# Attention loads issued in pairs of turns with a sixth home, and two weight rows converted later

## The chip, the cores and the metric

The kernel runs on one core of a Trainium2 chip. The metric is the device time of one execution in microseconds; the median of three runs is compared. One more execution was taken with a profile, and all rows below come from it.

## What is computed

Retention attention over 4 batches, 8 heads, 576 positions and head size 64, and behind it two feed-forward blocks on the 2304 tokens (model width 512, hidden width 2048), the first with a leaky ReLU whose slope is learnt, the second with a GELU in its sigmoid form:

```python
scores = scale * np.matmul(q, k.transpose(0, 1, 3, 2))
Dmat = np.where(rel >= 0, gamma[:, None, None] ** rel[None, :, :], 0.0)
ret = scores * Dmat[None, :, :, :]
attn = np.matmul(ret, v)
...
h = x @ w_in
g = np.maximum(h, 0.0) + alpha * np.minimum(h, 0.0)
x = g @ w_out
...
h = x @ w_in
g = h * (1.0 / (1.0 + np.exp(-1.702 * h)))
out = g @ w_out
```

The weights arrive as 64-bit floats in two 32-bit words each. The kernel puts them together itself and splits each value into a high and a low part, so that three products (high times high, high times low, low times high) replace one product in full precision.

## The kernel before

**Attention.** The 16 pairs of heads are worked on in turns, one pair a turn, in the loop `for i in range(n_a + 1)`; turn 16 only finishes pair 15. In turn `i` TensorE multiplies queries with keys (`a_scores`, tile `sc`), sums the keys' outer products with the values into a state (`a_outer`, tile `st`, needs the keys `kts` that ScalarE scaled in `a_keys` a turn before), and multiplies the scores of pair `i - 1` with its values (`a_within`, tile `av`). In an even turn it also does the last block of pairs `i` and `i + 1` (`a_tail`, which needs the inputs `ld` of pair `i + 1`) and adds the part that comes from earlier blocks for the two pairs before (`a_across`, tile `avt`). ScalarE takes the states out (`a_states`), and copies the finished outputs (`a_out`); VectorE multiplies the scores with the decay (`a_evac`), combines the states (`a_sums`), and for the first eight pairs writes the low part of the outputs (`a_rests`).

**Loads.** Each pair has two transfers on SyncE's queue: its inputs `ld` (864 KB; one of five homes, list `LOADS`), and its keys once more in another layout, `kts` (256 KB; one of eight places). `a_load` is called once a turn, four turns ahead. A home comes free when `a_across` has read its pair, which happens two pairs at a time in even turns; SyncE takes its instructions in order, so a transfer whose home is still in use holds up all behind it. The trace shows SyncE also waiting before an issue until a transfer eight places earlier has landed.

**Weight rows.** The first block's weights come in 16 rows. Row `m` is loaded in two pieces (`w_load`, `w_piece`, tile `raw`, two slots: `m % 2`) and converted by six instructions: ScalarE's `w_abs` (line 118, writes `cv`), VectorE's `w_clamp` (two instructions, lines 122 and 125), `w_top` (132) and `w_low` (139), ScalarE's `w_hi` (line 85, writes the high part of `w`), VectorE's `w_lo` (line 90, writes its low part). The third of every three products of a row needs the low part. A table of times says in which turn, or later in which step, each of these instructions is written into the program: `rows` for rows 0 to 2, `pace` for rows 3 to 15; `run_to(t)` emits what is due. Engines run their instructions in that order.

**First block.** Behind the attention, steps follow (`steps`): each multiplies one row's first weights with a chunk of 512 tokens (`mm1`, line 484, 12 products), ScalarE and VectorE make the activation (`activate`, lines 494 to 496, and `split`, lines 85 and 90), and two steps later TensorE multiplies it with the row's second weights (`mm2`, line 527). So TensorE does `mm1` of rows 0, 1 and 2 in a row, and then `mm2` and `mm1` in turn. Row 7 is needed for the first time in the eleventh step.

Of the kernel before, what the change touches and what calls it, by code (L numbers as in the profile page):

```python
# [7 lines left out]
F32 = mybir.dt.float32  # L8
# [15 lines left out]
SYNC = mybir.DependencyInfo(mybir.DependencyClass.Sync, mybir.DependencyReason.DATA)  # L24
F64_MIN = 2.0 ** -15
F64_MAX = 2.0 ** 17 * (1 - 2.0 ** -24)
LOADS = (4, 5, 6, 7, 10)
BLOCKS = [(0, 0, 0, 3), (0, 1, 0, 8), (0, 0, 3, 11), (0, 1, 8, NM), (0, 0, 11, NM)]
N_FIRST = len(BLOCKS)
BLOCKS += [(0, c, 0, NM) for c in (2, 4, 3)]  # L30
# [10 lines left out]
def kernel(  # L41
# [17 lines left out]
    def pool(name, bufs, **kw):  # L59
        return ctx.enter_context(tc.tile_pool(name=name, bufs=bufs, **kw))  # L60

    const = pool("const", 1)
    wp = pool("wp", 1)
# [174 lines left out]
    def rest_home(i):  # L238
# [3 lines left out]
            return xs_home[n // 2][:, 1728 + n % 2 * 128:1856 + n % 2 * 128]  # L242
        return xs_home[n // 3][:, n % 3 * S:n % 3 * S + S]

    def kts(i):
        return kts_t[i // 4 % 2][:, i % 4]

    def a_load(i):
        b, p = PAIRS[i]
# [488 lines left out]
    def after2(r, i, d):  # L738
# [30 lines left out]
    n_a = len(PAIRS)  # L769
    base = n_a + 1  # L770
    rows = (
        (2.8, 5.75, 7.0, 8.0, 9.0, 9.25, 10.0), (7.2, 9.75, 11.0, 12.0, 13.0, 13.25, 14.0),
        (11.0, 13.75, 15.0, 16.0, 16.1, 16.25, 16.6),
    )
    pace = [base] * len(rows)
    pace += [base + t for t in (0.8, 2.35, 3.9, 5.45, 7.0, 8.8, 10.6, 12.4, 14.2, 15.9, 17.6, 19.3, 21.4)]
    for m, t in enumerate(pace):
        times = rows[m] if m < len(rows) else [t + d for d in (-1.6, 0.0, 0.5, 1.0, 1.5, 1.75, 2.25)]
        at(times[0], w_load, (1, m), w1, m % 2)
# [5 lines left out]
    events.sort(key=lambda e: e[:2])  # L785

    with tc.manual_schedule():
        kts_t = [wp.tile([128, 4, 512], F32, tag=f"w{n}", name="kts") for n in (3, 11)]
        r_home = [wp.tile([128, 2048], F32, tag=f"w{n}", name="r") for n in (8, 9, 15)]
        xs_home = [wp.tile([128, 2048], F32, tag=f"w{n}", name="xs") for n in (12, 13, 14)]  # L790
        for t, a in ((fades_sb, fades), (vtab_sb, vtab)):
# [11 lines left out]
        def a_fill(n):  # L803
            for _ in range(n):
                nc.tensor.matmul(out=wps[:, 0:128], lhsT=wz, rhs=wz, start=True, stop=True)
# [8 lines left out]
        for i in range(n_a + 1):  # L814
            j = i - 1
            first = i % 2 == 0
            done = (i - 2, i - 1) if first and i else ()
            if i < n_a:
                a_scores(i)
                a_queries(i)  # L820
                if not first:
                    a_rests(i - 3)
                a_evac(i)
            if i in (1, 2):
                a_tables(i + 1)
            if not first:
                a_rests(i - 2)
            run_to(i)
            if 0 < i < n_a - 1:
                a_keys(i + 1)  # L830
            if i == 0:
                a_tail(0)
                a_fill(1)
            if i < n_a:
                a_outer(i)
            if i == 0:
                a_states(i)
                a_tables(1)
            if i != 1:
                a_within(max(j, 0))  # L840
            if i == 1:
                a_tail(1)
            elif first and 0 < i < n_a:
                a_tail(i)
                a_tail(i + 1)
            if 0 < i < n_a:
                a_states(i)
            if i < n_a:
                a_sums(i)
            if i == 0:  # L850
                a_keys(1)
                a_otab(1)
            run_to(i + 0.25)
            if done:
                a_across(done)
                for n in done:
                    a_out(n)
            if i in (1, 2):
                a_otab(i + 1)
            for n in (3, 4) if i == 0 else (i + 4,):  # L860
                if n < n_a:
                    a_load(n)
            if i == 0:
                nc.sync.dma_start(out=alpha_sb, in_=alpha)
            run_to(i + 0.75)
# [14 lines left out]
        for n, (_, c, m0, _) in enumerate(BLOCKS[N_FIRST:], 1):  # L880
            homes[c] = xp[n % 2]
            for k in range(NK):
                t = starts[c, m0] + (-4 + 0.9 * k, -4.4 + 0.9 * k, (-7.0, -6.2, -2.2, -1.7)[k])[n - 1]
# [171 lines left out]
```

## Time and profile before

| What | Value |
|---|---|
| median of 3 runs | 824.39 us (823.78 to 826.39) |
| the profiled execution | 826.13 us, of which the trace spans 824.4 us |
| TensorE busy | 98% of the span |
| VectorE busy | 76% |
| ScalarE busy | 56% |
| GpSimd busy | 4% |
| end of the attention on TensorE | 75.39 us from the span's start |
| first `mm2` | 83.70 us |

The span runs from the first to the last instruction of the trace; 1.7 us of the profiled execution's time lie outside it. The profiled execution stands 1.7 us above the median of the runs.

### The profile page before, as it was taken

What the parts mean: (1) busy time and instruction counts of PE and PEld (TensorE: products, weight loads), DVE (VectorE), ACT (ScalarE), POOL (GpSimd) and SP (SyncE); (2) the same over time, 40 slices, a digit from 0 to 9 for tenths busy, and PEclk for the clock granted to TensorE, in tenths of its full rate; (3) what the DMA queues carried; (4) which work ended last, traced back from release to release, by engine and by line L of the source; (5) the groups of instructions that cost most, each with busy time, mean ns of one, the idle gap of its engine ahead of it and who ended that gap; (6) DMA issues with size and microseconds to landing.
All of it is one profiled execution on the core that took longest, in us unless ns stands there. A gap on an engine that the chain in (4) does not pass through costs nothing.

```text
span 824.4 us, 14022 instructions
## 1 busy us (share of the span) xinstructions
PE 809.5 (98%) x5102; PEld 738.4 (90%) x5102; DVE 627.5 (76%) x1145; ACT 462.8 (56%) x939; POOL 36.4 (4%) x54
## 2 busy tenths in 40 slices
PE   8888999999999999999999999999999999999998
PEld 7777887888888888999888899999999999999998
DVE  6687887787585678678669887799777699677875
ACT  6555664554443435564455676676566566566653
POOL 1221000000001110010000000000000000000000
PEclk9999999999999999999999999999999999999999
DMA  8995743454165575764475454787544977445871
GB/s 306 357 313 180 248 154 116 138 185 177 53 226 190 182 227 149 253 192 138 164 247 161 165 180 135 285 292 256 177 129 131 353 260 260 135 132 206 290 269 72
DMA packets 65722, 166.61 MB, mean 202 GB/s; under 512 B 7155, under 2 KB 32755, under 8 KB 59894
## 3 DMA queue, kind: packets, MB, share of 16 engines
q1 hardware_dynamic: 60896, 148.93, 52.8%
q0 software_dynamic: 4608, 16.78, 6.9%
q8 instruction: 40, 0.66, 0.3%
q14 instruction: 28, 0.23, 0.1%
q10 hardware_dynamic: 150, 0.02, 0.0%
HBM read 128.48 MB, written 37.22 MB: 201 GB/s over the span
## 4 chain that ended last, share of the span: by engine, by line
PE 85%; DMA 7%; DVE 4%; ACT 2%; issue 1%; SPq 0%; DVEq 0%; ACTq 0%
PE acc L652 24%; PE acc L527 21%; PE h L484 21%; PE h L652 19%; DMA raw<-in_w_dram 4%; DMA ld<-in_qkv_dram 2%; PE av L297 1%; DMA kts<-in_kn_dram 1%; DVE cv L139 1%; DVE g L496 1%; DVE cv L132 1%; ACT cv L118 0%; DVE w L90 0%; ACT kts L261 0%; DVE gsf L90 0%
## 5 line engine op out<-in xcount | busy, mean ns | idle before, releaser
L484 PE MATMUL h<-x,w 128*128 128x512 f32 (+1 forms) x960 | 210.3, 368 | 0.5 <-DVE w L90 0.5
L527 PE MATMUL acc<-gsf,w 128*128 128x512 f32 (+1 forms) x960 | 209.8, 368 | 0.0
L85 ACT ACTIVATE gsf<-g 128x384 fp32r<-128x384 f32 (+2 forms) x248 | 133.3, 544 | 117.2 <-DVE g L496 72.3
L484 PEld LDWEIGHTS h<-x,w 128*128 128x128 f32 x960 | 168.2, 189 | 30.9 <-DVE w L90 0.9
L527 PEld LDWEIGHTS acc<-gsf,w 128*128 128x128 f32 x960 | 168.3, 189 | 30.0
L90 DVE TENSOR_TENSOR gsf<-g,gsf 128x384 fp32r<-128x384 f32 (+2 forms) x248 | 141.1, 577 | 49.5 <-ACT gsf L85 48.5
L496 DVE SCALAR_TENSOR_TENSOR g<-h,nalpha_sb,g 128x512 f32<-128x512 f32 (+1 forms) x80 | 55.6, 695 | 67.4 <-ACT h L495 67.3
L652 PE MATMUL acc<-x,ws 128*128 128x384 f32 x552 | 106.8, 334 | 0.0
L652 PE MATMUL acc<-gsf,ws 128*128 128x384 f32 x576 | 101.3, 334 | 0.0
L652 PEld LDWEIGHTS acc<-gsf,ws 128*128 128x128 f32 x576 | 100.0, 188 | 0.0
L652 PEld LDWEIGHTS acc<-x,ws 128*128 128x128 f32 x552 | 96.7, 188 | 0.0
L652 PE MATMUL h<-x,ws 128*128 128x384 f32 x456 | 90.3, 334 | 0.0
L494 ACT ACTIVATE g<-h 128x512 f32<-128x512 f32 (+1 forms) x80 | 43.9, 549 | 71.8 <-PE h L484 71.8
L652 PEld LDWEIGHTS h<-x,ws 128*128 128x128 f32 x456 | 80.1, 188 | 0.1
L652 PE MATMUL h<-gsf,ws 128*128 128x384 f32 x432 | 77.0, 335 | 0.1
L652 PEld LDWEIGHTS h<-gsf,ws 128*128 128x128 f32 x432 | 74.9, 188 | 0.9 <-DVE gsf L90 0.8
L555 DVE TENSOR_TENSOR tm<-h,tm 128x384 f32<-128x384 f32 x73 | 40.5, 555 | 31.9 <-PE h L652 27.7
L90 DVE TENSOR_TENSOR ws<-rw,ws 128x512 fp32r<-128x512 f32 x96 | 56.9, 615 | 0.0
L555 DVE TENSOR_TENSOR g<-g,g 128x384 f32<-128x384 f32 x93 | 51.3, 551 | 0.7
L85 ACT ACTIVATE ws<-rw 128x512 fp32r<-128x512 f32 x96 | 49.8, 569 | 0.0
L118 ACT ACTIVATE cv<-raw 128x1024 f32<-128x1024 f32 x32 | 36.1, 1128 | 16.2 <-DMA raw<-in_w_dram 14.5
L495 ACT ACTIVATE h<-h 128x512 f32<-128x512 f32 (+1 forms) x80 | 43.9, 549 | 0.0
(90 smaller groups left out, 707.3 us busy)
## 6 DMA issues: line engine op xcount, KB each, us to landing
ws<-sg SPq DMA_DIRECT2D x42, 1024.0 KB, 5.9
raw<-in_w_dram SPq DMA_DIRECT2D x32, 512.0 KB, 5.0
raw<-in_w_dram POOLq DMA_DIRECT2D x32, 512.0 KB, 5.2
rw<-rg SPq DMA_DIRECT2D x24, 512.0 KB, 3.5
ld<-in_qkv_dram SPq DMA_DIRECT2D x13, 864.0 KB, 7.8
rw<-rg SPq DMA_DIRECT2D x24, 384.0 KB, 3.1
sg<-sums SPq DMA_DIRECT2D x40, 128.0 KB, 2.4
kts<-in_kn_dram SPq DMA_DIRECT2D x16, 256.0 KB, 7.3
```

Of the source, the lines that this page charges most:

```text
L85: return nc.scalar.activation(out=out, in_=in_, func=ACTF.Copy)
L90: latest[0] = eng.tensor_tensor(out=out, in0=a, in1=b.bitcast(F32), op=ALU.subtract)
L118: nc.scalar.activation(out=cvs[key], in_=raws[key][:, :, 1].bitcast(F32), func=ACTF.Abs)
L132: latest[0] = nc.vector.scalar_tensor_tensor(out=g, in0=raws[key][:, :, 1], scalar=-(1 << 30), in1=g, op0=ALU.bitwise_and, op1=ALU.bitwise_or,
L139: latest[0] = nc.vector.scalar_tensor_tensor(out=g, in0=raws.pop(key)[:, :, 0], scalar=29, in1=g, op0=ALU.logical_shift_right, op1=ALU.bit ...
L484: nc.tensor.matmul(out=t, lhsT=w[:, cw, k * 128:k * 128 + 128], rhs=x[:, cx], start=(i == 0), stop=(i == 3 * NK - 1),)
L494: nc.scalar.activation(out=g, in_=t, func=ACTF.Relu)
L495: nc.scalar.activation(out=t, in_=t, func=ACTF.Relu, scale=-1.0)
L496: nc.vector.scalar_tensor_tensor(out=g, in0=t, scalar=nalpha_sb[:, m:m + 1], in1=g, op0=ALU.mult, op1=ALU.add)
L527: nc.tensor.matmul(out=acc[0][d], lhsT=w[:, cw, d * 128:d * 128 + 128], rhs=g[:, cx], start=(m == m0 and i == 0), stop=(m == m1 - 1 and i ...
L555: nc.vector.tensor_tensor(out=out, in0=x, in1=y, op=op)
L652: nc.tensor.matmul(out=out, lhsT=w(cw), rhs=x(cx), start=(start and n == 0), stop=True, skip_group_check=True,)
```

## The change

The inputs get a sixth home (`w11`, which held four of the keys' places); the keys get six places in all, four in `w3` and two in a half of an attention work tile that nothing else uses. Pairs 3, 4 and 5 are loaded in turn 0, and from then on two pairs are loaded together in each even turn: pairs `i + 4` and `i + 5`. Weight row 1 is loaded at turn 10.8 instead of 7.2 and row 2 at 10.9 instead of 11.0, which puts both behind the loads of pair 15; their conversion is written later, that of row 2 mostly behind the attention. Rows 3 to 7 move by 0.1 to 0.4 steps. One filling product in turn 0 is dropped.

```diff
--- before.py
+++ after.py
@@ -24,7 +24,7 @@
 SYNC = mybir.DependencyInfo(mybir.DependencyClass.Sync, mybir.DependencyReason.DATA)
 F64_MIN = 2.0 ** -15
 F64_MAX = 2.0 ** 17 * (1 - 2.0 ** -24)
-LOADS = (4, 5, 6, 7, 10)
+LOADS = (4, 5, 6, 7, 10, 11)
 BLOCKS = [(0, 0, 0, 3), (0, 1, 0, 8), (0, 0, 3, 11), (0, 1, 8, NM), (0, 0, 11, NM)]
 N_FIRST = len(BLOCKS)
 BLOCKS += [(0, c, 0, NM) for c in (2, 4, 3)]
@@ -242,8 +242,10 @@
             return xs_home[n // 2][:, 1728 + n % 2 * 128:1856 + n % 2 * 128]
         return xs_home[n // 3][:, n % 3 * S:n % 3 * S + S]
 
+
     def kts(i):
-        return kts_t[i // 4 % 2][:, i % 4]
+        i %= 6
+        return kts_home[:, i] if i < 4 else r_home[2][:, 1024 + (i - 4) * 512:1536 + (i - 4) * 512]
 
     def a_load(i):
         b, p = PAIRS[i]
@@ -769,11 +771,11 @@
     n_a = len(PAIRS)
     base = n_a + 1
     rows = (
-        (2.8, 5.75, 7.0, 8.0, 9.0, 9.25, 10.0), (7.2, 9.75, 11.0, 12.0, 13.0, 13.25, 14.0),
-        (11.0, 13.75, 15.0, 16.0, 16.1, 16.25, 16.6),
+        (2.8, 5.75, 7.0, 8.0, 9.0, 9.25, 10.0), (10.8, 13.75, 14.0, 14.75, 15.25, 15.5, 16.0),
+        (10.9, 16.25, 16.7, 17.1, 17.5, 17.75, 18.25),
     )
     pace = [base] * len(rows)
-    pace += [base + t for t in (0.8, 2.35, 3.9, 5.45, 7.0, 8.8, 10.6, 12.4, 14.2, 15.9, 17.6, 19.3, 21.4)]
+    pace += [base + t for t in (1.2, 2.75, 4.3, 5.7, 7.1, 8.8, 10.6, 12.4, 14.2, 15.9, 17.6, 19.3, 21.4)]
     for m, t in enumerate(pace):
         times = rows[m] if m < len(rows) else [t + d for d in (-1.6, 0.0, 0.5, 1.0, 1.5, 1.75, 2.25)]
         at(times[0], w_load, (1, m), w1, m % 2)
@@ -785,7 +787,7 @@
     events.sort(key=lambda e: e[:2])
 
     with tc.manual_schedule():
-        kts_t = [wp.tile([128, 4, 512], F32, tag=f"w{n}", name="kts") for n in (3, 11)]
+        kts_home = wp.tile([128, 4, 512], F32, tag="w3", name="kts")
         r_home = [wp.tile([128, 2048], F32, tag=f"w{n}", name="r") for n in (8, 9, 15)]
         xs_home = [wp.tile([128, 2048], F32, tag=f"w{n}", name="xs") for n in (12, 13, 14)]
         for t, a in ((fades_sb, fades), (vtab_sb, vtab)):
@@ -830,7 +832,6 @@
                 a_keys(i + 1)
             if i == 0:
                 a_tail(0)
-                a_fill(1)
             if i < n_a:
                 a_outer(i)
             if i == 0:
@@ -857,7 +858,7 @@
                     a_out(n)
             if i in (1, 2):
                 a_otab(i + 1)
-            for n in (3, 4) if i == 0 else (i + 4,):
+            for n in (3, 4, 5) if i == 0 else (i + 4, i + 5) if first else ():
                 if n < n_a:
                     a_load(n)
             if i == 0:
```

On SyncE's queue, before, from pair 11's keys to the end of the loads (`ld_634` is pair 11 and `ld_870` pair 15; `raw_632` is weight row 1, `raw_845` row 2):

```order
L255 DMA kts_124<-in_kn_dram 128x512
L114 DMA raw_632<-in_w1_dram 128x1024
L253 DMA ld_709<-in_qkv_dram 128x1728
L255 DMA kts_125<-in_kn_dram 128x512
L253 DMA ld_753<-in_qkv_dram 128x1728
L255 DMA kts_125<-in_kn_dram 128x512
L253 DMA ld_827<-in_qkv_dram 128x1728
L255 DMA kts_125<-in_kn_dram 128x512
L114 DMA raw_845<-in_w1_dram 128x1024
L253 DMA ld_870<-in_qkv_dram 128x1728
L255 DMA kts_125<-in_kn_dram 128x512
L114 DMA raw_845<-in_w1_dram 128x1024
```

and now, from pair 12 (`ld_704`) to the two rows (`raw_839` is row 1, `raw_841` row 2):

```order
L255 DMA ld_704<-in_qkv_dram 128x1728
L257 DMA kts_124<-in_kn_dram 128x512
L255 DMA ld_707<-in_qkv_dram 128x1728
L257 DMA kts_124<-in_kn_dram 128x512
L255 DMA ld_820<-in_qkv_dram 128x1728
L257 DMA kts_124<-in_kn_dram 128x512
L255 DMA ld_823<-in_qkv_dram 128x1728
L257 DMA kts_124<-in_kn_dram 128x512
L114 DMA raw_839<-in_w1_dram 128x1024
L114 DMA raw_841<-in_w1_dram 128x1024
L114 DMA raw_839<-in_w1_dram 128x1024
L114 DMA raw_841<-in_w1_dram 128x1024
```

The pieces of the weight rows no longer stand between the pairs; row 1's second piece is the third transfer behind the keys of pair 15.

On ScalarE, before, from the time of turn 14 to the conversion of row 2 (`w_980` is row 1, `cv_982` and `w_1103` row 2; `kts_125` are the keys of pair 15):

```order
L118 ACTIVATE cv_982<-raw_845 128x1024
L261 ACTIVATE kts_125<-kts_125,vtab_sb_78 128x4x64 x2
L261 ACTIVATE r_128<-st_1000,vtab_sb_78 128x320
L85 ACTIVATE xs_130<-av_967 128x512
L85 ACTIVATE xs_130<-avt_1027 128x64
L85 ACTIVATE xs_130<-av_1009 128x512
L85 ACTIVATE xs_130<-avt_1028 128x64
L261 ACTIVATE r_126<-st_1020,vtab_sb_78 128x320
L85 ACTIVATE w_1103<-cv_982 128x1024
```

and now (`cv_972` and `w_1080` are row 1, `cv_1092` row 2; `kts_124` are the keys of pair 15):

```order
L118 ACTIVATE cv_972<-raw_839 128x1024
L263 ACTIVATE kts_124<-kts_124,vtab_sb_78 128x4x64 x2
L263 ACTIVATE r_127<-st_991,vtab_sb_78 128x320
L85 ACTIVATE xs_129<-av_959 128x512
L85 ACTIVATE xs_129<-avt_1018 128x64
L85 ACTIVATE xs_129<-av_1000 128x512
L85 ACTIVATE xs_129<-avt_1019 128x64
L263 ACTIVATE r_125<-st_1011,vtab_sb_78 128x320
L85 ACTIVATE w_1080<-cv_972 128x1024
L118 ACTIVATE cv_1092<-raw_841 128x1024
```

In the place ahead of the keys of pair 15 where row 2's `w_abs` stood, now row 1's stands; row 2's comes behind the last state.

On VectorE, before, from row 2's `w_top` to the activation of the second step (`w_1103` is row 2, `g_1155` and `g_1181` the activations of steps 0 and 1):

```order
L132 SCALAR_TENSOR_TENSOR cv_982<-raw_845,cv_982 128x1024
L139 SCALAR_TENSOR_TENSOR cv_982<-raw_845,cv_982 128x1024
L90 TENSOR_TENSOR w_1103<-cv_982,w_1103 128x1024
L866 TENSOR_SCALAR nalpha_sb_84<-alpha_sb_83 128x16
L496 SCALAR_TENSOR_TENSOR g_1155<-h_1142,nalpha_sb_84,g_1155 128x512
L90 TENSOR_TENSOR gsf_1141<-g_1155,gsf_1141 128x512
L496 SCALAR_TENSOR_TENSOR g_1181<-h_1161,nalpha_sb_84,g_1181 128x512
L122 TENSOR_SCALAR cv_1177<-cv_1177 128x1024
```

and now, from row 1's `w_low` (`cv_972`, `w_1080`) on; `cv_1092` and `w_1169` are row 2, `g_1148` and `g_1173` the activations of steps 0 and 1:

```order
L139 SCALAR_TENSOR_TENSOR cv_972<-raw_839,cv_972 128x1024
L90 TENSOR_TENSOR w_1080<-cv_972,w_1080 128x1024
L122 TENSOR_SCALAR cv_1092<-cv_1092 128x1024
L125 TENSOR_SCALAR cv_1092<-cv_1092 128x1024
L867 TENSOR_SCALAR nalpha_sb_84<-alpha_sb_83 128x16
L498 SCALAR_TENSOR_TENSOR g_1148<-h_1135,nalpha_sb_84,g_1148 128x512
L132 SCALAR_TENSOR_TENSOR cv_1092<-raw_841,cv_1092 128x1024
L139 SCALAR_TENSOR_TENSOR cv_1092<-raw_841,cv_1092 128x1024
L90 TENSOR_TENSOR gsf_1134<-g_1148,gsf_1134 128x512
L498 SCALAR_TENSOR_TENSOR g_1173<-h_1156,nalpha_sb_84,g_1173 128x512
L90 TENSOR_TENSOR w_1169<-cv_1092,w_1169 128x1024
L90 TENSOR_TENSOR gsf_1134<-g_1173,gsf_1134 128x512
```

All of row 2's conversion used to stand ahead of the first activation. Now its `w_clamp` stands ahead of it, its `w_top` and `w_low` behind it, and its `w_lo` behind the second activation.

## Rows read from the trace of the kernel before

**Rows 1.** What TensorE waited for, 4.5 to 75.39 us (total, times, longest).

```profile
PE av L297 <- DVE x L90: 3.2, 4, 1.2
PE st L297 <- ACT kts L261: 3.0, 3, 1.1
PE st L297 <- DMA ld<-in_qkv_dram: 2.7, 4, 0.9
```

**Rows 2.** The same, from 75.5 us to the end.

```profile
PE h L484 <- DVE w L90: 0.5, 1, 0.5
```

**Rows 3.** Critical chain to 130 us: issue and time to landing of three transfers.

```profile
6.57 9.78 DMA ld<-in_qkv_dram
...
17.79 6.77 DMA ld<-in_qkv_dram
...
61.33 6.67 DMA raw<-in_w_dram
```

**Rows 4.** Stretches of the attention: busy us of engines, then clock, DMA share, GB/s.

```profile
8.00:16.00 8.00, 7.75 (x120) 6.73 (x116) 6.10 (x18) 5.85 (x17) 2.81 (x3) 1.00 1.04 414
...
26.00:34.00 8.00, 7.47 (x156) 6.67 (x158) 5.57 (x14) 3.40 (x10) 2.29 (x2) 1.00 0.92 315
...
42.43:50.98 8.55, 7.08 (x150) 6.19 (x144) 8.48 (x16) 3.68 (x10) 2.63 (x3) 1.00 0.86 297
```

**Rows 5.** Timeline of ScalarE: start, us, what [idle before <- releaser].

```profile
33.66 1.13 ACT L118 ACTIVATE cv<-raw 128x1024 f32<-128x1024 f32 x1 [4.42 <-DMA raw<-in_w_dram]
...
68.08 1.12 ACT L118 ACTIVATE cv<-raw 128x1024 f32<-128x1024 f32 x1 [2.75 <-DMA raw<-in_w_dram]
...
79.43 0.62 ACT L494 ACTIVATE g<-h 128x512 f32<-128x512 f32 x1
...
89.72 1.06 ACT L85 ACTIVATE w<-cv 128x1024 fp32r<-128x1024 f32 x1 [0.50 <-DVE cv L139]
```

**Rows 6.** Timeline of TensorE, same columns.

```profile
37.56 1.09 PE L297 MATMUL av<-r,ld 128*64 128x128 f32 x16 [1.25 <-DVE x L90]
...
49.83 0.27 PE L297 MATMUL st<-ld 64*64 64x64 f32 x2 [0.59 <-DMA ld<-in_qkv_dram]
...
50.98 1.16 PE L297 MATMUL sc<-ld 64*128 64x128 f32 x16
...
59.47 1.41 PE L297 MATMUL sc<-ld 64*128 64x128 f32 x16
...
66.23 0.27 PE L297 MATMUL st<-ld 64*64 64x64 f32 x2 [0.89 <-DMA ld<-in_qkv_dram]
...
67.38 1.16 PE L297 MATMUL sc<-ld 64*128 64x128 f32 x16
...
75.39 8.47 PE L484 MATMUL h<-x,w 128*128 128x512 f32 x36
...
83.70 2.88 PE L527 MATMUL acc<-gsf,w 128*128 128x512 f32 x12
...
125.64 2.58 PE L484 MATMUL h<-x,w 128*128 128x512 f32 x10 [0.51 <-DVE w L90]
```

**Rows 7.** Timeline of VectorE, same columns.

```profile
70.44 0.42 DVE L366 SCALAR_TENSOR_TENSOR r<-r,vtab_sb 128x192 f32<-128x192 f32 x1 [2.90 <-ACT r L261]
...
80.63 0.75 DVE L496 SCALAR_TENSOR_TENSOR g<-h,nalpha_sb,g 128x512 f32<-128x512 f32 x1 [0.92 <-ACT h L495]
...
86.67 1.22 DVE L132 SCALAR_TENSOR_TENSOR cv<-raw,cv 128x1024 int32<-128x1024 int32 x1
...
87.81 0.74 DVE L496 SCALAR_TENSOR_TENSOR g<-h,nalpha_sb,g 128x512 f32<-128x512 f32 x1
...
88.47 1.22 DVE L139 SCALAR_TENSOR_TENSOR cv<-raw,cv 128x1024 int32<-128x1024 int32 x1
...
91.79 0.75 DVE L496 SCALAR_TENSOR_TENSOR g<-h,nalpha_sb,g 128x512 f32<-128x512 f32 x1 [0.17 <-ACT h L495]
...
124.37 1.21 DVE L90 TENSOR_TENSOR w<-cv,w 128x1024 fp32r<-128x1024 f32 x1
```

## The prediction

> **What bounds the kernel now.** I read the waits of TensorE first, split at the end of the attention. Up to 75.39 us it waits 8.9 us: for the low parts of the outputs, for scaled keys and for loaded inputs [rows 1]. From there to the end it waits 0.5 us [rows 2]. So whatever moves the first `mm2`, which begins at 83.70 [rows 6], moves the end one to one, and a wait added behind the attention costs its full length. Next, what stands behind the 8.9 us. The critical chain runs through transfers [rows 3], and ScalarE waits 4.42 and 2.75 us in front of `w_abs` for a weight row [rows 5], with the keys of the next pair and the states queued behind it. The stretches show why the transfers are late: with a full queue 414 GB/s arrive, later 315 and 297 [rows 4], because a pair's issue waits for a home and the queue runs dry: pair 5, issued at 17.79, needed 6.77 us to land [rows 3], of which its 864 KB account for 2.1 at 414 GB/s. A start on a dry queue thus costs about 4.6 us. Last, VectorE: from 42.43 to 50.98 it is busy 8.48 of 8.55 us [rows 4], so there the loads don't decide.
>
> **The queue to turn 10 (gain).** Pair 3's inputs land at 16.35 (6.57 + 9.78) [rows 3], in both kernels. One pair is 1120 KB, 2.8 us at 414 GB/s. Pair 5 now stands right behind pair 4: pair 3's keys, pairs 4 and 5 are 2.56 MB, 6.2 us, so pair 5 is there at 22.5 and not at 24.56 or later. Pairs 6 and 7 and both pieces of row 0 (3.34 MB, 8.1 us) follow without a gap and end at 30.6; I take 31.0. Before, ScalarE got row 0 at 33.66 [rows 5], and TensorE's wait of 1.25 us at 37.56 [rows 6] hangs on that through states, sums and low parts. So turn 7 and all behind it comes 2.6 us earlier. Bounds: nothing, if transfers keep to 315 GB/s (5.9 MB from 16.35 end at 35.1), and 3.6 if row 0 lands at 30.0. In turns 7 to 10 the full VectorE neither adds to this nor takes from it; its instructions there are the same. The wait for pair 11's inputs at 49.83, 0.59 us [rows 6], goes too, since that pair is issued a turn earlier and no piece of row 1 stands ahead of it. Turn 11 began at 50.98 [rows 6]; now at 50.98 - 2.6 - 0.6 = 47.8.
>
> **Turns 11 to 14.** Turns 13 and 14 took 67.38 - 59.47 = 7.91 us, 0.89 of it a wait for pair 15 [rows 6]. Without waits two turns take 7.0, so turn 15 begins at 47.8 + 14.0 = 61.8 (before: 67.38).
>
> **Row 1 arrives late (a wait that moves).** The homes of pairs 14 and 15 come free only at the end of turn 10, 47.8. Behind them stand row 1's first piece, row 2's first and row 1's second. The two pairs and three pieces are 3.87 MB, 9.3 us at 414 GB/s. With the dry queue's 4.6 us they end at 61.7; with a queue that still holds some of pairs 12 and 13, at 58.8. Those pairs were issued some 8 us before and need 5.6, so the queue is nearly dry: I take 60.7. ScalarE reaches row 1's `w_abs` at the end of turn 13, some 4 us earlier, and behind it stand pair 15's keys and pair 14's state, as behind row 2's `w_abs` before. That one began at 68.08 and the attention ended 7.31 us later [rows 5, 6]. Now `w_top` (1.14 us, 86.67 to 87.81 [rows 7]) stands between the sums that began at 70.44 [rows 7] and the scores of pair 15, and `w_clamp` no longer behind those scores, which I estimate to give back 0.65. That makes 7.8 us: the attention ends at 60.7 + 7.8 = 68.5, 6.9 earlier.
>
> **Row 2 behind the attention (loss).** Before, row 2 was ready in time. Now its `w_top` and `w_low` wait behind the first activation, its `w_hi` holds up the second one on ScalarE, and its `w_lo` waits behind that second one on VectorE. From the attention's end: a `mm1` takes (83.70 - 75.39) / 3 = 2.77 us [rows 6], so ScalarE starts the first activation at about 3.0; VectorE 1.20 later (79.43 to 80.63 [rows 5, 7]), 4.2; `w_top` 0.66 later (87.81 to 88.47 [rows 7]), 4.9; `w_low` 1.14 later, 6.0; `w_hi` 1.25 later (88.47 to 89.72 [rows 7, 5]), 7.25; the second activation on VectorE 2.07 later (89.72 to 91.79 [rows 5, 7]), 9.3; `w_lo` 0.66 later, 10.0; and TensorE's third product of row 2 another 1.27 later (124.37 to 125.64 [rows 7, 6]), 11.3. Without a wait that product would begin at 6.0 (two `mm1` and two products). TensorE waits 5.3 us, about half ahead of the high part and half ahead of the low one. I see no work that hides this: its next instructions are in order behind it. Bounds: 4.5 if the first activation starts as soon as its product is done and each hand-over is 0.1 shorter, 5.9 if ScalarE comes late from row 1's `w_hi`, row 2's `w_abs` and four copies. The first `mm2` comes 8.31 + 5.3 = 13.6 after the attention: at 82.1 instead of 83.70. Gain 1.6.
>
> **Row 7.** The wait of 0.51 at 125.64 [rows 6] was VectorE's backlog. VectorE gets about 5 us more behind the attention (three instructions of 1.2 and the two of `w_clamp`), TensorE 5.3 us later; so the wait should go: 0.5, at least nothing. Rows 3 to 7 move by up to 0.4 steps, which lies inside this. The dropped filling product costs nothing as long as turn 2 waits for the landing at 16.35 anyway.
>
> **Sum.** 1.6 + 0.5 = 2.1 us: the profiled span goes from 824.4 to 822.3, the profiled execution from 826.13 to 824.0, and the median of the runs, 1.7 us below the latter, from 824.39 to 822.3.
>
> **Rivals.**
> - *The transfers stay slow (slower than before).* If the queue keeps to 315 GB/s [rows 4] although it is fuller, row 0 comes no earlier, turn 11 begins at 50.4, row 1's second piece lands at 50.4 + 4.6 + 12.3 = 67.3, the attention ends at 75.1, and the 5.3 us of row 2 stand almost alone: 829. It decides where the attention ends later than 70.6, that is row 1 after 62.8. For it: the rate was low at a DMA share of 0.92 [rows 4]. Against: the queue ran dry in those stretches, and 414 were moved when it did not.
> - *Row 1 lands in time.* If ScalarE doesn't wait for it, turn 15 runs from 61.8 without its waits (8.0 us, of which I put 3 down to them) and the attention ends at 66.8: 820.6. It needs row 1 some 2 us earlier than the flow bound of 58.8 gives.
> - *TensorE's clock falls in the wait for row 2.* The granted clock is 1.00 in all stretches shown, with no wait over 1.25 us [rows 1, 4, 6]; here TensorE stands still twice for over 2.5 us with two products between. At 1.2 GHz instead of 2.4 the ten remaining products (2.3 us) take twice as long, and the `mm2` behind them (2.8 us) too: 2.3 to 5.1 us more, 824.6 to 827.4. The Trainium skill ("TensorE: Matmul & The Clock Gate", section "Why this matters for your kernels") warns of this: idle gaps between bursts of matmuls put the engine back to the lower clock. By that rule the price is the one just given; no wait in this trace is long enough to show it.
>
> **How the numbers follow.** I give the forecast 0.50 (its own range 820.8 to 824.0, from the bounds of row 1's landing and of the wait for row 2), slow transfers 0.15, row 1 in time 0.17, the clock 0.18. Runs of this kernel tell 0.3%, 2.5 us, from no change: 821.9 to 826.9 counts as the same. Of the forecast 0.20 lie below that and 0.30 inside; of slow transfers 0.11 above and 0.04 inside; of row 1 in time 0.16 below, 0.01 inside; of the clock 0.06 above and 0.12 inside. So faster 0.36, same 0.47, slower 0.17. The range of 819.8 to 827.2 leaves out a tail of the early row 1 and most of the slow transfers.
>
> **What would show it.** In the profile of the changed kernel: pair 5's inputs issued near 10 us; ScalarE at row 0's `w_abs` near 31 and no wait for pair 11; ScalarE waiting some 3 us for row 1 near 60; the attention's end at 67 to 70; the 36 products of `mm1` broken by two waits of 2 to 3 us for row 2, and `mm2` 13 to 14 us behind the attention; no wait at row 7. The prediction is wrong if that gap is near 8 us, if the granted clock drops there, or if the attention ends after 71.

## The result

The changed kernel takes 833.15 us (median of 4 runs, 832.60 to 834.61), the kernel before, measured beside it, 824.62: a ratio of 1.0103, 95% interval 1.0081 to 1.0125. It is 8.5 us slower; 822.3 was forecast, and 827.2 was the upper end of the range. The profiled execution of the changed kernel spans 830.9 us (before: 824.4). Behind line 245 its lines stand two further down: `mm1` is line 486, `mm2` line 529.

The attention did become shorter. First, what TensorE waits for from 4.5 to 67.5 us, against [rows 1] (total, times, longest):

```profile
PE av L299 <- DVE x L90: 2.7, 3, 1.3
PE av L299 <- DVE r L339: 1.3, 1, 1.3
PE st L299 <- ACT kts L263: 1.3, 2, 0.7
PE av L299 <- ACT xs L85: 0.2, 1, 0.2
```

It waits 5.5 us in place of 8.9, and none of that is for a pair's inputs. That is 3.4 of the 7.95 us by which the attention ends earlier (below). Most of the rest are products that keep TensorE busy for less time: 57.16 us from 4.5 us to the attention's end, before 61.08, for nearly the same number of products. 1.4 us of that lies ahead of pair 3's scores (11.01 us busy there, before 12.39), where the clock stands at 1.00 from 7.9 us on and before only from 11.4; the cause of the rest is not shown. Two stretches of the attention, against [rows 4]; the last three columns are clock, DMA share and GB/s:

```profile
17.60:31.00 13.40, 12.77 (x272) 11.39 (x272) 9.96 (x25) 7.58 (x19) 4.57 (x4) 1.00 1.02 415
31.00:46.00 15.00, 12.50 (x266) 10.97 (x269) 13.71 (x28) 9.56 (x28) 4.15 (x4) 1.00 0.95 364
```

The queue now stays full to 31 us, at 415 GB/s. Then the timeline of TensorE from the attention's end to row 7 (start, us, what, count, [idle before <- what ended it]), against [rows 6]:

```profile
67.14 0.30 PE L299 MATMUL avt<-r,ld 64*64 64x64 f32 x8
70.65 5.74 PE L486 MATMUL h<-x,w 128*128 128x512 f32 x24 [3.21 <-ACT xs L85]
79.23 0.98 PE L486 MATMUL h<-x,w 128*128 128x512 f32 x2 [2.84 <-ACT w L85]
82.12 4.52 PE L486 MATMUL h<-x,w 128*128 128x512 f32 x10 [1.91 <-DVE w L90]
86.48 2.93 PE L529 MATMUL acc<-gsf,w 128*128 128x512 f32 x12
...
130.82 4.10 PE L486 MATMUL h<-x,w 128*128 128x512 f32 x10 [2.88 <-DVE w L90]
134.75 1.53 PE L529 MATMUL acc<-gsf,w 128*128 128x512 f32 x6
```

The attention ends at 70.65 - 3.21 = 67.44, 7.95 us earlier than before. Behind it TensorE stands still four times; before, it ran through and waited once, 0.51 us [rows 6]. The ten products at 82.12 take 4.52 us and those at 130.82 take 4.10, where ten took 2.58 [rows 6]. Two windows give the reason (busy us of the engines, then the granted clock):

```profile
79.54:86.36 6.82, 4.91 (x12) 3.41 (x11) 3.78 (x5) 2.17 (x4) 0.00 (x0) 0.50 0.99 335
130.74:134.15 3.41, 3.33 (x8) 2.65 (x9) 1.76 (x3) 0.00 (x0) 0.00 (x0) 0.50 0.00 0
```

In both the granted clock is 0.50, which is 1.2 GHz; at all other times from 7.9 us until the last products are done it is 1.00.

The account, in the profiled executions, against before:

| Place | us |
|---|---|
| end of the attention, 75.39 to 67.44 | -7.95 |
| first `mm1` waits for the copy `xs` | +3.21 |
| row 2: 2.84 for the high part, 1.91 for the low part | +4.75 |
| low clock from 79.54, and the breaks: first `mm2` at 86.48, less 67.44, 8.31 without waits [rows 6], 3.21 and 4.75 | +2.77 |
| first `mm2` to the one behind row 7: 134.75 - 86.48 = 48.27, before 128.05 - 83.70 = 44.35 | +3.92 |
| sum | +6.70 |

The last row takes from before this line:

```profile
128.05 2.88 PE L527 MATMUL acc<-gsf,w 128*128 128x512 f32 x12
```

The spans differ by 6.5. Of the 2.77 about 2.2 are the low clock: two and ten products take 0.98 and 4.52 us, where they take 0.73 and 2.60 at a clock of 1.00, broken in the same places (the run with the waits filled, below). The other 0.6 come from the breaks themselves. In the last row 2.37 are the longer wait (2.88 in place of 0.51), the other 1.55 the low clock. The medians differ by 8.5, because before's profiled execution is a long one among its own: 826.13 us, 1.5 above its median, while 832.65 for the changed one is 0.5 below. Nor is all of the 7.95 the change's: the scores of pair 3 begin at 15.51 us here and at 17.63 before, 2.12 us earlier, and that start differs from one execution to the next (below).

The row that was not foreseen is the second. ScalarE at that place:

```profile
59.47 1.14 ACT L118 ACTIVATE cv<-raw 128x1024 f32<-128x1024 f32 x1 [4.22 <-DMA raw<-in_w_dram]
...
67.32 1.06 ACT L85 ACTIVATE w<-cv 128x1024 fp32r<-128x1024 f32 x1 [3.89 <-DVE cv L139]
68.28 1.12 ACT L118 ACTIVATE cv<-raw 128x1024 f32<-128x1024 f32 x1
...
70.37 0.23 ACT L85 ACTIVATE xs<-avt 128x64 f32<-128x64 f32 x1
73.76 0.60 ACT L496 ACTIVATE g<-h 128x512 f32<-128x512 f32 x1 [3.17 <-PE h L486]
```

Row 1's `w_hi` and row 2's `w_abs` stand ahead of the copies of the last pair's outputs, and the first `mm1` begins when the last copy is done. Why it should wait for that copy, the memory places in the built programs tell (numbers of PSUM banks):

```
           sc, pair 15   avt, pair 15   h of mm1 for rows 0, 1, 2
before     0 and 1       2              0, 3, 2
changed    2 and 1       0              0, 3, 2
```

The filling product of turn 0 writes a tile in bank 0, one of three banks in which `sc` and one of each two `avt` take turns. Without it that tile is free sooner, pair 1's first scores take its bank, and from there on banks 0 and 2 change places in all later tiles of this kind. `avt` of the last pair then lies where the first `h` is to be written, so the first `mm1` waits until `avt` has been copied; before, it was the third `mm1` that needed that bank, when the copy was done. Theory A: this dropped product, the late row 2 and the later times of rows 3 to 7 each bring a wait, and the clock falls behind the waits. The rivals: the waits only take each other's place (B); the clock or the loads themselves are to blame; the late rows are needed for the gain of the attention.

### The profile page after: what moved, and what is told of

It is laid out like the page before. It is cut to its first block, busy times and chain, and to the rows that moved or that the text cites. A ratio compares the mean times of both kernels' runs of the same rounds, so it can differ in the third digit from the quotient of the medians.

```text
span 830.9 us, 14021 instructions
## 1 busy us (share of the span) xinstructions
PE 809.9 (97%) x5100; PEld 738.4 (89%) x5100; DVE 628.1 (76%) x1145; ACT 462.7 (56%) x939; POOL 36.6 (4%) x54
## 4 chain that ended last, share of the span: by engine, by line
PE 89%; DVE 4%; DMA 3%; ACT 2%; issue 1%; SPq 0%; DVEq 0%; ACTq 0%
PE acc L654 24%; PE h L486 22%; PE acc L529 22%; PE h L654 19%; DMA raw<-in_w_dram 2%; DMA kts<-in_kn_dram 1%; PE av L299 1%; PE sc L299 1%; DVE cv L139 1%; DVE w L90 1%; DVE cv L132 1%; DVE r L339 1%; DMA ld<-in_qkv_dram 0%; PE st L299 0%; DVE g L498 0%
## 5 line engine op out<-in xcount | busy, mean ns | idle before, releaser
L486 PE MATMUL h<-x,w 128*128 128x512 f32 (+1 forms) x960 | 214.6, 373 | 10.8 <-DVE w L90 4.8
L486 PEld LDWEIGHTS h<-x,w 128*128 128x128 f32 x960 | 170.5, 191 | 43.1 <-DVE w L90 5.9
```

The lines of the kernel that those rows point to most:

```text
L486: nc.tensor.matmul(out=t, lhsT=w[:, cw, k * 128:k * 128 + 128], rhs=x[:, cx], start=(i == 0), stop=(i == 3 * NK - 1),)
```

## Experiments: the dropped filling product

**The kernel before without the product.**

```diff
-                a_fill(1)
```

> The kernel before without the filling product of turn 0, and nothing else. Theory A: the first mm1 waits from the attention's end, 75.4, until the copy of the last avt is done, which before was at 79.57: 4.2 us, 828.6 us if the clock stays at 1.0, up to 831 if it falls behind that wait. Rival B: the product is worth nothing or the ScalarE copies come sooner: 824.4 (824 to 825.5). On the start: if the dropped product is also why the first turns of the changed kernel ran 1 to 2 us earlier, the scores of pair 3 begin near 15.5 instead of 17.6 here too, and 1 to 2 us less are lost.

Measured: 832.07 us, ratio 1.0083 (1.0058 to 1.0109), so 6.5 us for one product of 128 columns. TensorE, and the window of the low clock:

```profile
76.33 0.29 PE L297 MATMUL avt<-r,ld 64*64 64x64 f32 x8
80.42 11.02 PE L484 MATMUL h<-x,w 128*128 128x512 f32 x36 [3.80 <-ACT xs L85]
91.27 1.07 PE L527 MATMUL acc<-gsf,w 128*128 128x512 f32 x4
```

```profile
79.14:85.97 6.83, 5.55 (x13) 4.40 (x14) 1.31 (x2) 1.22 (x5) 0.00 (x0) 0.50 0.94 319
```

A wait of 3.80 us for `xs`, and 36 products that take 11.02 us in place of 8.47 [rows 6]: 3.80 + 2.55 = 6.35 us behind the attention, where the medians differ by 6.5. (In this profile the attention itself ends 1.2 us later than before, at 76.62, with the clock at 0.50 from 72.32 to 75.73 too; this execution is 1.8 us above the run's median.) Theory A holds in its dearer form. The scores of pair 3 begin at 16.36 here. Over all profiles of this document they begin at 15.51 to 17.65: at 16.36 to 17.65 with the old way of loading (three profiles), at 15.51 to 17.57 with the new one (eleven). Without the filling product it is 15.51 to 17.42 (six), with it 16.48 to 17.65 (eight). So neither the loads nor the product is shown to set that start, and up to 2.1 of the 7.95 us above can belong to the two executions and not to the change.

**The changed kernel with the product put back.**

```diff
                 a_tail(0)
+                a_fill(1)
```

> The changed kernel with the filling product of turn 0 put back, and nothing else. Theory A (banks): that product takes a turn in the rotation of the three banks of sc; without it the last pair's avt lies in the bank of the first mm1's h, and the first mm1 waits 3.2 us for the copy of avt. With it back, the first mm1 begins within 0.2 us of the attention's end, ScalarE reaches the first activation 3 us earlier, row 2's chain hangs on that activation, so the first mm2 comes about 3 us earlier too (13.6 to 16.4 us behind the attention, depending on the clock): 830.0 us (829 to 831). Rival B (the wait only moves): row 2's conversion is bound by something else than the first activation, the two waits for row 2 grow by the same 3 us and the time stays at 833. On the clock: if the two waits for row 2 are enough to lower it, the granted clock falls to 0.5 behind them here as well; if it needs the 3.2 us in front, it stays at 1.0 and the time is 827.5.

Measured: 831.22 us, ratio 1.0071 (1.0050 to 1.0091).

```profile
67.96 5.75 PE L486 MATMUL h<-x,w 128*128 128x512 f32 x24
76.56 0.73 PE L486 MATMUL h<-x,w 128*128 128x512 f32 x2 [2.85 <-ACT w L85]
79.45 4.63 PE L486 MATMUL h<-x,w 128*128 128x512 f32 x10 [2.16 <-DVE w L90]
83.88 1.29 PE L529 MATMUL acc<-gsf,w 128*128 128x512 f32 x3
...
128.94 4.15 PE L486 MATMUL h<-x,w 128*128 128x512 f32 x10 [3.09 <-DVE w L90]
```

The wait of 3.21 us is gone and the two for row 2 stay (5.01), so the waits do not take each other's place; the first `mm2` comes 2.6 us earlier, 3.1 counted from the attention's end (15.92 us behind it, 19.04 in the changed kernel). The ratios too lie 0.0032 or 2.6 us apart, less than the 3.2 expected, and their intervals overlap. The clock falls behind row 2's waits here too.

**The copies first.** Row 1's `w_hi` and `w_lo` at 16.3 and 16.31, row 2's `w_abs` at 16.32, all behind the copies; banks as changed.

```diff
-... 14.75, 15.25, 15.5, 16.0),
-... (10.9, 16.25, 16.7, ...
+... 14.75, 15.25, 16.3, 16.31),
+... (10.9, 16.32, 16.7, ...
```

> The changed kernel with row 1's w_hi and row 2's w_abs behind the four copies of the last outputs on ScalarE, where they stand ahead of them; the banks stay as the change left them. Theory A: the first mm1 waits for the last copy because of the bank, and that copy is late because of the two instructions ahead of it; with the copies first it is done about 1.7 us behind the attention's end, the first mm1 waits 1.6 us in place of 3.2, and the first mm2 comes 1.6 us earlier: 831.5 us (830.5 to 832.5). Rival: the copies wait for something else and the first mm1 still begins 3.2 us behind the attention's end.

Measured: 832.34 us, ratio 1.0084 (1.0069 to 1.0099).

```profile
69.43 5.76 PE L486 MATMUL h<-x,w 128*128 128x512 f32 x24 [1.17 <-ACT xs L85]
```

The first `mm1` waits 1.17 us in place of 3.21 and begins at 69.43, so the order on ScalarE sets the length of the wait and the bank makes it. By the ratios that is 1.6 us, as expected, but the intervals alone would not tell it from the changed kernel.

**Row 2 converted at the times of before, the rest as changed.**

```diff
-(10.9, 16.25, 16.7, 17.1, 17.5, 17.75, 18.25)
+(10.9, 13.75, 15.0, 16.0, 16.1, 16.25, 16.6)
```

> The changed kernel with row 2 converted at the times of before (w_abs at 13.75 to w_lo at 16.6), everything else as changed. Theory: the waits for row 2 (2.84 and 1.91 us) go, and with them the low clock from 79.5 to 86.4; the first mm1 still waits for the copy of avt, some 4 us now, because row 2's w_hi stands ahead of that copy on ScalarE, and the attention ends 1 us later because of w_abs: the first mm2 at about 81 in place of 86.5, 827.6 us (826.5 to 829). Rival C (the clock answers to any long wait): the wait of 4 us at the first mm1 alone lowers the clock, and some 2.5 us come back: 830. Rival D: row 2 in time costs the attention more than 3 us on ScalarE and VectorE, and nothing is won: 832 to 833.

Measured: 834.99 us, ratio 1.0126 (1.0108 to 1.0143): 7.4 us above what was expected. The waits for row 2 did go, but the one for the bank grew to 7.64 us:

```profile
78.32 9.89 PE L486 MATMUL h<-x,w 128*128 128x512 f32 x36 [7.64 <-ACT xs L85]
```

```profile
76.01 1.06 ACT L85 ACTIVATE w<-cv 128x1024 fp32r<-128x1024 f32 x1 [3.69 <-DVE cv L139]
...
78.03 0.24 ACT L85 ACTIVATE xs<-avt 128x64 f32<-128x64 f32 x1
```

Row 2's `w_hi` waits for VectorE until 76.01, and the copies stand behind it. I had put 4 us there from the order alone. The clock is low three times in this profile (64.31 to 67.72, 74.55 to 81.37, 132.57 to 139.40), the first within the attention and the last at row 7, where TensorE still waits 3.09 us. It is also the first hint that row 1's late load is a fault of its own: the two rows' `w_abs` now follow each other ahead of the keys of pair 15, TensorE waits 3.14 us for those, and the attention ends at 70.68. (The profiled execution, 837.30 us, is 2.3 above the run's median.)

## Experiments: row 7

**Rows 3 to 7 at the times of before, the rest as changed.**

```diff
-... (1.2, 2.75, 4.3, 5.7, 7.1, 8.8, ...
+... (0.8, 2.35, 3.9, 5.45, 7.0, 8.8, ...
```

> The changed kernel with the times of rows 3 to 7 as before, everything else as changed. Theory: the wait for row 7 grew from 0.51 to 2.88 us because the later times put its conversion behind other work on VectorE and ScalarE; with the old times it is at most 1 us, the clock stays at 1.0 there, and 3 to 3.9 us come back: 829.5 us (829 to 830.5). Rival: it grew because row 2's conversion now lies behind the attention and ScalarE and VectorE never catch up; then the wait stays near 2.9 us, the clock falls again, and the time stays at 833.

Measured: 832.23 us, ratio 1.0080 (1.0055 to 1.0105). The wait at row 7 is gone, and from the first `mm2` to the one behind row 7 it is 134.74 - 90.69 = 44.05 us in place of 48.27. So the later times made that wait, not row 2's work on VectorE. Yet the end comes no earlier, because in this run the clock fell during the wait for the copy, and again at row 2:

```profile
71.31 8.64 PE L486 MATMUL h<-x,w 128*128 128x512 f32 x24 [3.21 <-ACT xs L85]
82.36 0.73 PE L486 MATMUL h<-x,w 128*128 128x512 f32 x2 [2.41 <-ACT w L85]
86.26 4.64 PE L486 MATMUL h<-x,w 128*128 128x512 f32 x10 [3.16 <-DVE w L90]
90.69 1.53 PE L529 MATMUL acc<-gsf,w 128*128 128x512 f32 x5
```

```profile
70.66:77.49 6.83, 6.18 (x15) 4.83 (x16) 1.02 (x3) 1.19 (x4) 0.00 (x0) 0.50 0.27 106
84.31:91.14 6.83, 4.88 (x12) 3.87 (x13) 4.92 (x6) 0.78 (x2) 0.00 (x0) 0.50 0.84 313
```

So what row 7 gave back is lost ahead of it: the first `mm2` is at 90.69 where the changed kernel has it at 86.48. Most of these 4.2 us are the clock's (24 products take 8.64 us in place of 5.74); the waits for row 2 are 0.8 longer, and the attention ends 0.7 later. The interval overlaps that of the changed kernel: a gain in time from these edits is not shown here.

**Row 7's time alone put back, 7.0 for 7.1.**

```diff
-... 5.7, 7.1, 8.8, ...
+... 5.7, 7.0, 8.8, ...
```

> The changed kernel with one number put back: row 7's time, 7.0 in place of 7.1. Theory: events are written out only at whole and half steps, so the 0.1 puts row 7's w_abs, w_clamp, w_top and w_low each half a step later (7.0, 7.5, 8.0 and 8.5 become 7.1 to 8.6), and its w_lo (9.35) behind row 8's w_clamp (9.3); with 7.0 the wait of 2.88 us at row 7 is at most 1 us and the clock stays at 1.0 there: 829.5 us (828.5 to 830.5). Rival: the wait comes from the sum of all the later rows on VectorE, row 2's included; it stays above 2 us, and the time at 832.5 or more.

Measured: 834.32 us, ratio 1.0129 (1.0105 to 1.0153). My theory failed: TensorE waits 0.71 us one row earlier and still 2.15 us at row 7, together as much as in the changed kernel. The clock did stay at 1.00 there.

```profile
124.89 2.60 PE L486 MATMUL h<-x,w 128*128 128x512 f32 x10 [0.71 <-DVE w L90]
132.82 2.58 PE L486 MATMUL h<-x,w 128*128 128x512 f32 x10 [2.15 <-DVE w L90]
```

It takes the times of rows 3 to 6 as well; which of them, no run here tells.

## Experiments: the clock

**The product and the times of rows 3 to 7 put back.** What is left are the loads and the late rows 1 and 2: what the forecast took the change to come to.

```diff
+                a_fill(1)
-... (1.2, 2.75, 4.3, 5.7, 7.1, 8.8, ...
+... (0.8, 2.35, 3.9, 5.45, 7.0, 8.8, ...
```

> The changed kernel with the filling product and the old times of rows 3 to 7: what is left of the change is the loads and the late rows 1 and 2, the scene that the forecast was worked out for. Theory: first mm1 right behind the attention's end (67.8), two waits of 5.0 us together for row 2, clock at 0.5 behind them (2.6 us), no wait at row 7: the first mm2 at 83.9, the median at 825 (824 to 826.5). Rival H: the wait for row 7 comes back without the bank wait that gave VectorE time, 828 to 829. If the clock stayed at 1.0, 822.5.

Measured: 828.98 us, ratio 1.0040 (1.0024 to 1.0057). No wait at the bank, none at row 7; the clock is at 0.50 from 66.69 to 70.11 and from 80.35 to 87.17, the first of these within the attention, which ends at 70.26. The waits for row 2 are 2.84 and 3.17, and the first `mm2` is at 87.17:

```profile
78.83 0.73 PE L486 MATMUL h<-x,w 128*128 128x512 f32 x2 [2.84 <-ACT w L85]
82.73 4.60 PE L486 MATMUL h<-x,w 128*128 128x512 f32 x10 [3.17 <-DVE w L90]
```

That is the upper rival of this run's expectation in time, but not by its mechanism.

**The same, with the waits filled.** 21 products that nobody reads, 12 ahead of row 2's first product, 9 ahead of its third.

```diff
+                if (c, m) == (0, 2) and i in (0, 2):
+                    hold(9 if i else 12)
```

> As the run with the filling product and the old times, and 21 products of 512 columns more, which nobody reads (into a bank that is free until the first mm2): 12 ahead of row 2's first product, 9 ahead of its third, 4.8 us at full clock, where TensorE otherwise stands still for 5.0 us. Theory: the waits themselves are not shortened, but the clock stays at 1.0 to the first mm2, which comes at 81.3 to 81.7 in place of 83.9; 822.5 us. Rival: the clock has not to do with these waits and falls all the same; then the filling products take longer than the waits and the time is 826 to 829.

Measured: 825.99 us (10 runs), ratio 1.0003 (0.9992 to 1.0014), 3.0 us less than without them; the two intervals do not meet.

```profile
73.16 2.88 PE L483 MATMUL hold<-x,w 128*128 128x512 f32 x12
76.19 0.73 PE L495 MATMUL h<-x,w 128*128 128x512 f32 x2 [0.15 <-ACT w L85]
76.77 2.21 PE L483 MATMUL hold<-x,w 128*128 128x512 f32 x9
80.09 2.60 PE L495 MATMUL h<-x,w 128*128 128x512 f32 x10 [1.11 <-DVE w L90]
82.53 1.75 PE L538 MATMUL acc<-gsf,w 128*128 128x512 f32 x7
```

```profile
67.00:84.00 17.00, 15.73 (x96) 12.40 (x89) 11.84 (x16) 9.79 (x17) 0.00 (x0) 1.00 0.64 209
```

The clock stays at 1.00 and ten products take 2.60 us again. Row 2's third product begins 12.5 us behind the attention's end in both profiles (80.09 less 67.59; 82.73 less 70.26), so row 2 is ready no sooner, and yet the first `mm2` comes 14.94 us behind it in place of 16.91: 2.0 us, the price of the clock there. The last us of the 3.0 is not shown to come from the filled waits: in the profile without them the clock had fallen ahead of these waits too, within the attention, and the attention ended 2.7 us later. Over all executions of the two runs the mean clock is 0.994 to 0.996 without the filling products and 0.997 to 1.000 with them. The time is 3.5 us above the 822.5 expected: the first `mm2` comes 14.94 us behind the attention (67.59), not 13.6, since with the old times row 3's `w_abs` (1.10 us) stands ahead of the second activation on ScalarE, and row 2's `w_lo` behind that (row 2's third product comes 12.5 us behind the attention's end, 11.5 with the product back and the changed times); and a wait of 0.9 us for a later activation turns up. The remaining 1.3 us of the miss stay open.

## Experiments: the loads and the late rows

**The loads alone**, in the kernel before: six homes, six places for the keys, two pairs at a time. All row times and the filling product as before.

```diff
-LOADS = (4, 5, 6, 7, 10)
+LOADS = (4, 5, 6, 7, 10, 11)
...
-            for n in (3, 4) if i == 0 else (i + 4,):
+            for n in (3, 4, 5) if i == 0 else (i + 4, i + 5) if first else ():
```

> The kernel before with the loads of the change alone: six homes, the keys' six places, loads in pairs of turns. The filling product, the times of all rows and of row 1's load (7.2, ahead of pairs 12 and 13) stay as before. Theory: the loads are the part that gains; the attention ends some 7 us earlier than 75.4, the first mm2 comes 8.3 us behind it, row 7 waits 0.5 us, the clock stays at 1.0: 817.5 us (816.5 to 819.5). Rival F (row 1's place pays for it): with row 1 ahead of pairs 12 and 13 these land 2.5 us later, the attention ends at 71 to 72, 821. Rival G: the steps behind the attention are tuned to the old hand-over; a wait of 2 to 3 us turns up at a later row and lowers the clock, 822 or more.

Measured: 817.08 us, ratio 0.9901 (0.9884 to 0.9919): 7.9 us faster than before, as expected.

```profile
67.23 0.28 PE L299 MATMUL avt<-r,ld 64*64 64x64 f32 x4
67.44 8.47 PE L486 MATMUL h<-x,w 128*128 128x512 f32 x36
75.75 2.88 PE L529 MATMUL acc<-gsf,w 128*128 128x512 f32 x12
...
117.89 2.56 PE L486 MATMUL h<-x,w 128*128 128x512 f32 x10 [0.63 <-DVE w L90]
```

The attention ends at 67.44, to the hundredth where it ends in the changed kernel, though pair 3's scores begin 1.07 us later (16.58, there 15.51), and the first `mm2` follows 8.31 us behind, as before. Row 1 and row 2, loaded at their old places, hold up ScalarE nowhere:

```profile
46.34 1.23 ACT L118 ACTIVATE cv<-raw 128x1024 f32<-128x1024 f32 x1
...
60.01 1.25 ACT L118 ACTIVATE cv<-raw 128x1024 f32<-128x1024 f32 x1
```

Both begin without idle time before them. So these profiles show nothing that the late rows gave the attention.

**Loads, and row 1 late, row 2 in time.** The changed kernel with the product, the times of rows 3 to 7 and row 2's conversion of before.

```diff
-... (7.2, 9.75, 11.0, 12.0, 13.0, 13.25, 14.0),
-... (11.0, 13.75, 15.0, ...
+... (10.8, 13.75, 14.0, 14.75, 15.25, 15.5, 16.0),
+... (10.9, 13.75, 15.0, ...
```

(against the run with the loads alone)

> The changed kernel with the filling product, the old times of rows 3 to 7 and row 2 converted at the times of before: what is left are the loads and row 1's late load and conversion. Theory: the attention ends at 70.5 as in the run with row 2's old times, the copy of the last avt is done 7.6 us behind it, because row 2's w_hi stands ahead of it on ScalarE, but that copy now holds up only the third mm1, which is due 5.6 us behind the attention's end: one wait of 2 us, first mm2 at 81, 821.5 to 822.5. Rival: with row 2's conversion in the attention and row 1 late, VectorE falls behind and row 2's low part comes late as well: 824 or more.

Measured: 824.81 us (10 runs), ratio 0.9997 (0.9986 to 1.0008). Of the 7.9 us that the loads gave, 0.2 are left. The first `mm2` is at 81.24 as expected, but not by the expected wait of 2 us: TensorE waits 2.75 us for keys up to 63.81, the clock falls, and the attention ends at 71.74, 4.3 us later than with the loads alone.

```profile
63.24:73.48 10.24, 9.33 (x92) 7.86 (x93) 7.65 (x13) 4.00 (x10) 1.14 (x1) 0.50 0.10 26
```

**The late rows alone**, in the kernel before: times of rows 1 to 7 as changed, loads and product as before.

```diff
-... (7.2, 9.75, 11.0, 12.0, 13.0, 13.25, 14.0),
-... (11.0, 13.75, 15.0, 16.0, 16.1, 16.25, 16.6),
-... (0.8, 2.35, 3.9, 5.45, 7.0, 8.8, ...
+... (10.8, 13.75, 14.0, 14.75, 15.25, 15.5, 16.0),
+... (10.9, 16.25, 16.7, 17.1, 17.5, 17.75, 18.25),
+... (1.2, 2.75, 4.3, 5.7, 7.1, 8.8, ...
```

> The kernel before with the times of rows 1 to 7 as changed, and nothing else: loads one pair a turn, five homes, the filling product kept. Theory: the parts add up. Attention's end about 74 (rows 1 and 2 no longer hold up ScalarE in front of pairs 12 to 14, pair 15 comes later), the waits for row 2 with the low clock put the first mm2 16.2 us behind it, at 90 in place of 83.7, and row 7's wait with the low clock adds 4.7: 835 us (832 to 837). By sums: the change gave +8.5, the loads alone -7.9, the dropped product alone +6.5, which leaves +9.9 for the rows, 835. Rival: the late rows help the attention as much as they cost behind it, and the time is 827 or less.

Measured: 838.08 us, ratio 1.0155 (1.0136 to 1.0174), 12.0 us slower than before. The attention ends at 75.08, 0.3 earlier; the waits for row 2 are 2.87 and 1.67, at row 7 2.92, and the clock is low in three places, the first within the attention (38.63 to 42.05), so what the late rows do to the attention's end is not cleanly read here. The three parts alone are -7.9, +6.5 and +12.0, together +10.6; all at once they gave +8.5.

**The loads alone, and row 0 later.** The loads alone, and row 0's `w_abs` a turn later, where ScalarE waited 4.40 us for the row.

```diff
-... (2.8, 5.75, 7.0, ...
+... (2.8, 6.75, 7.0, ...
```

> The kernel before with the loads of the change alone (817.1 us), and row 0's w_abs a turn later (6.75 in place of 5.75). In the run with the loads alone ScalarE waits 4.40 us for row 0 at 30.89, keys and states stand behind it, and TensorE waits 0.79 us for keys and 1.24 us for low parts in turn 7. Theory: with w_abs later these 2 us go, the turns behind follow, since the later loads hang on homes that these turns free: 815.5 us (815 to 816.5). Rival I: VectorE is full from there to turn 10 and the 2 us return as a wait for low parts: 817.

Measured: 816.57 us, ratio 0.9890 (0.9870 to 0.9909). In its profile the attention ends at 64.95, 2.5 us earlier than with the loads alone, and the waits of 0.79 and 1.24 are gone, but its four runs lie between 815.07 and 817.64 and the profiled one is the fastest: beside the loads alone, the gain of 0.5 us is not shown. Both versions are faster than the kernel before and than the changed one.

## Why the prediction was wrong

**"The queue to turn 10" and "Turns 11 to 14": right.** Pair 5 was issued at 9.37, row 0 came at 29.72 (31.0 forecast), the rate was 415 GB/s, turn 11 began at 46.26 (47.8) and turn 15 at 59.28 (61.8). The rival of slow transfers did not come. But luck is in these times: the forecast had pair 3's inputs land at 16.35 in both kernels, and in this execution they landed at 14.22 (14.22 to 16.36 over all profiles).

**"Row 1 arrives late": right in place, the size in part by luck.** ScalarE waits 4.22 us and starts at 59.47 (60.7 forecast); the attention ends 7.97 us later (7.8), 7.95 earlier than before (6.9). Of the 7.95 the earlier start of pair 3 is 2.12; from pair 3's scores on it is 5.8, a little less than forecast. The 4.6 us for a start on a dry queue were read from pair 5 of before, but when that pair was issued, at 17.79, pair 4's keys were still on their way (they landed at 19.68), so the queue was not dry. Here the two pairs and three pieces took 12.99 us, from the issue at 46.40 to row 1's second landing at 59.39, that is 3.7 more than the 9.3 of their bytes. What I did not ask was what the attention would do with row 1 at its old place: it ends at 67.44 there too, and nothing comes behind it.

**"Row 2 behind the attention": right.** 4.75 us (5.3; bounds 4.5 to 5.9), and 5.01 with the product put back. With the old times of rows 3 to 7 as well it is 6.01, above the bounds, since row 3's `w_abs` then stands ahead of the second activation.

**"The dropped filling product costs nothing": wrong, the step that failed first.** I looked at when the product runs, not at which tile it keeps in use. The forecast put it at nothing; it cost 3.21 us of waiting in the changed kernel, and 6.5 us alone, clock included. The Trainium skill ("Perfetto Trace Analysis", section "Matmuls") says that independent groups of matmuls should rotate through different PSUM banks, so that the copy out of one runs beside the products of the next. The row at 70.65 agrees: with the same bank the products begin when the copy is done; with another one (67.96, product put back) they do not wait.

**"Row 7: the wait should go": wrong.** It grew from 0.51 to 2.88 us, and cost 3.92 with the clock. My working counted VectorE's work and held shifts of 0.1 to 0.4 steps for small. The run with the old times of rows 3 to 7 has no such wait; in its median the gain is not clear of noise.

**The clock: a rival with 0.18 that came, and more than once.** About 2.2 us behind row 2 (2.77 with the breaks; its bounds were 2.3 to 5.1), and 1.55 more at row 7, where I expected no wait at all; filling the waits of row 2 gave back 3.0 us in the median, 2.0 of them seen behind the attention. The rule of the Trainium skill ("TensorE: Matmul & The Clock Gate", section "Why this matters for your kernels") that idle gaps between bursts put the engine back agrees with these rows in the main, but not at each gap: behind the 3.21 us for the copy the clock stayed at 1.00. I gave the rival little because the waits of before, 1.25 us at most, had not lowered the clock, which says nothing against it.

**The sum.** With the attention's 7.95 in place of 6.9, and 3.21, 4.75, 2.77 and 3.92 behind it, the span grows by 6.7. Taking the median 1.7 us below the profiled execution was one more slip, of about 2 us: that distance belonged to one execution of before (the changed kernel's median is 0.5 above its own).

**Open.** Which of the times of rows 3 to 6 makes row 7 late, and why the parts alone add up to 2.1 us more than the whole. In all these runs the clock falls at places that differ from run to run (below), so I take sums of single parts to be good to some 2 us, an estimate.

## What to carry to other kernels

Price a change made of several parts part by part, and then ask of each part what the others would do without it: here the loads alone gain 7.9 us, and the late rows, which were to make room for them, and the dropped product lose more than all of it. Before an instruction is dropped, look at what it holds as well as at what it takes: the last reader or writer of a tile in a pool that goes round can decide in which bank all later tiles lie. A wait on TensorE can be charged twice, once for its length and once for the products that then run at the lower clock; where the wait could not be removed, products that nobody reads saved the second charge here.

## What the runs showed of the hardware

The same wait does not lower TensorE's clock in each execution. Through the wait of 3.21 us for the copy and the 24 products behind it the clock stayed at 1.00 in the changed kernel's profile; with the old times of rows 3 to 7 it fell within that wait (at 70.66; the wait ends at 71.31), and with row 7's time alone too (at 70.79; 71.14). With the late rows alone it fell in the midst of the attention, where the longest waits just ahead were of 1.21, 1.08 and 1.25 us:

```profile
38.63:42.05 3.42, 3.42 (x40) 2.87 (x38) 3.35 (x8) 1.09 (x3) 0.13 (x1) 0.50 0.78 319
```

Executions of the kernel before itself, measured beside the experiments, have mean clocks of 0.994 to 1.000 over the span, though the profiled one shows 1.00 from 11.4 us on. The time at which the clock first rises differs as well: 7.9 us in the changed kernel, 11.4 before, 8.2 to 12.8 in the others.
